# Where a chunk's state sums stand among the products of a Mamba-2 and MLP kernel on one core

## The chip, the core and the metric

The kernel runs on one core of one Trainium2 chip. A core has five engines that run side by side, each through its own queue in order: TensorE (PE in the profile; its weight loads are shown apart as PEld), VectorE (DVE), ScalarE (ACT), GpSimd (POOL) and the queue that issues transfers (SP). TensorE writes its products into PSUM, eight banks of 128 partitions by 512 fp32 words; VectorE and ScalarE read them there; everything else lies in SBUF. The metric is the time of one execution on the device, in microseconds, as the median of several runs.

## What is computed

A state-space layer (batch 4, 8 heads, 768 tokens, head size 32, state size 16) is followed by an MLP with a hardswish (256 to 2048 to 256), all in fp32 (the MLP's weights come as float64):

```python
for c in range(nc):                       # chunks of tokens
    cum = np.cumsum(la, axis=-1)          # la: log of the decay a
    L = np.exp(cum[:, :, :, None] - cum[:, :, None, :]) * causal
    M = np.einsum('bhin,bhjn->bhij', Cc, Bc) * L
    y_intra = np.einsum('bhij,bhjd->bhid', M, xc)
    y_inter = np.einsum('bhin,bhnd->bhid', Cc, state) * np.exp(cum)[..., None]
    y[:, :, sl] = y_intra + y_inter
    state = decay_full * state + sum_j(decay_from_j * Bc_j * xc_j)
...
h = x @ w_in                              # x: y with heads side by side
g = h * np.clip(h + 3.0, 0.0, 6.0) / 6.0
out = g @ w_out
```

## The kernel before

The tokens are cut into six chunks of 128 per sequence (NC = 6), all four sequences at once, and each chunk into two halves of 64 tokens (index `a`). Six stages `k` run the MLP of chunk `k`; into each one the attention of the next chunk, `c = k + 1`, is woven. The whole order is written out by hand: the engines' queues hold the instructions in the order in which the program emits them, and only waits for data or for buffers come on top.

The attention of a chunk has these parts, each with its line in the profile:
- `scores` (L530): C times B for each pair of heads, into four PSUM banks f0 to f3, named cb. Its products use the array in tiles of 32 rows and 64 columns (32*64).
- `from_state(c, a)` (L503): C times a state, into the output y. Half 0 uses the state left by the chunk before (`state`), half 1 the state at the middle of the chunk (`mid`). 32 products, 32*64.
- `into_state` (L544): the state sums, B weighted with the decay (`bs`) times x, 32 products for a half, in tiles of 64 rows and 32 columns (64*32). They go into `sps[c]`, the second halves of the banks y0 and y1 (the first halves hold y of half 0). The profile calls these tiles y as well.
- `multiply` (L574, VectorE): L times the scores, four instructions, which frees f0 to f3.
- `new_state` (L554, VectorE, two instructions): makes `mid` from the sums of half 0 and `tmp`, the decayed old state (L403, GpSimd); in `renew`, with `later` (L587) and the copy `adds` of the sums of half 1 (`take`, L560, ScalarE), it makes the chunk's last `state`.
- `mix` (L604): L times x into y, 128 products, 64*32, half `u` of the heads by half; y of token half 1 lies in the banks f0 and f1 (`y2`).
- `split_y` (L683, L684, L686): ScalarE and VectorE take y apart into three fp32r parts, y_hi, y_lo and y_less, the first layer's operands.

Stage `k` has two spans. In the first, for f from 2 to 15, the first layer's products (L694) and the activation follow each other, with hidden blocks rotating through the banks f0 to f3, y0 and y1. In the second, `wide_units` gives the second layer as products of whole-array tiles (L893, 128*128) into the banks wa, wb (pool ps_o) and wc (f2), cut into fourteen units of eight products (as the profile counts them); VectorE and ScalarE add the three banks together (L933, L934, L945, L946, L952, L953, L961) and the results are turned (L907) and stored (L914). L946 reads wb, and the products of unit 12 go on adding to wb behind it. After unit `i` the loop may emit parts of the next chunk's attention:

```python
if i == (3 if c == TURN else 2):          # TURN = 2
    scores(c); multiply(c)                # and renew(c), for TURN at i == 4
if ahead < NC and 3 <= i < 7:
    decay_ends(ahead, i - 3)              # ScalarE's L385, GpSimd's bs, L396
if i == 6 and c in (TURN, TURN + 1):
    mix(c, (0,))
if i == (7 if c in (TURN, TURN + 1) else 6):
    results(c, ...)                       # mix and split_y
```

So in stages 1 to 4, small products of chunks 2 to 5 stand in TensorE's queue between whole-array products. `scores` also emits `from_state(c, 0)` and `into_state`, for chunk 2 half 0 only (half 1 follows at unit 4, in `renew`), for chunk 5 half 0 only (its last state isn't needed). For chunk 5 `from_state(5, 0)` is emitted after unit 1, ahead of its scores. At unit 9 VectorE turns the B and C of the chunk after next (`turn_all`: L465, L475, L481); after `results`, ScalarE raises the decay of the chunk after next (`from_start`, L389), and SP loads the decays of the chunk behind that (`rows`: L301, L308). GpSimd also sums gT for the second layer (`g_sums`, L797) and masks the decays (L158).

Buffers that matter: `bs`, `mid`, `tmp`, `adds`, `later` and `xt` have one buffer; `state`, `L` and `eto` (the decay from a chunk's start) have two.

Of the kernel before, what the change touches and what calls it, by code (L numbers as in the profile page):

```python
# [8 lines left out]
FP32 = mybir.dt.float32  # L9
# [12 lines left out]
def kernel(  # L22
# [25 lines left out]
    P = 128  # L48
    NB, NH, S, D = x.shape
    N = B.shape[-1]  # L50
    DM, DF = moe_w_in.shape[0], moe_w_out.shape[0]
    NC = S // P
# [6 lines left out]
    HT = P // 2  # L59
# [24 lines left out]
    TURN = 2  # L84
# [431 lines left out]
    def scores(c):  # L516

        bT, cT, _ = bTs[c]
        cbs[c] = [ps.tile([P, NB, 2, HT], FP32, name="cb", tag=f"f{q}") for q in range(NQ)]
        if c not in ys:
            own_banks(c)
        for b in range(NB):
            for a, rows in enumerate(HALF):
                for q in range(NQ):
                    pair = slice(32 * q, 32 * q + 32)
                    nc.tensor.matmul(  # L530
                        out=cbs[c][q][rows, b], lhsT=bT[pair, b, rows],
                        rhs=cT[pair, b, :, rows], start=(b == 0), stop=True,
                        tile_position=(32 * q, a * HT), skip_group_check=True)
        if c == TURN:
            from_state(c, 0)
        into_state(c, *range(2 if c not in (TURN, NC - 1) else 1))

    def into_state(c, *halves):
        xt, bs = xts[c], bss[c]
        for b in range(NB):  # L540
            for q in range(NQ):
                hs = slice(b * NH + 2 * q, b * NH + 2 * q + 2)
                for a in halves:
                    nc.tensor.matmul(  # L544
                        out=sps[c][a][32 * q:32 * q + 32, b],
                        lhsT=bs[HALF[a], hs].rearrange("s h n -> s (h n)"),
                        rhs=xt[HALF[a], hs].rearrange("s h d -> s (h d)"),
                        start=(c == 0 and b == 0), stop=True, tile_position=(a * HT, 32 * q),
                        skip_group_check=True)

    def new_state(t, sp, old):
        for u in range(2):
# [8 lines left out]

    def multiply(c):

        if c < NC - 1 and c != TURN:
            take(c)
        mids[c] = mid = att.tile([P, NB, 2 * D], FP32, name="mid", bufs=1)
        if c == 0:
            for t in range(2):
                nc.scalar.activation(
                    mid[:, :, t * D:(t + 1) * D], sps[c][0][:, :, t * D:(t + 1) * D], AF.Copy,  # L570
                    scale=parity[:, t:t + 1])
        for q in (2, 0, 1, 3) if c in (TURN, NC - 1) else range(NQ):
            hs = slice(2 * q, 2 * q + 2)
            nc.vector.tensor_tensor(  # L574
                out=Ls[c][:, :, hs], in0=Ls[c][:, :, hs], in1=cbs[c][q], op=ALU.mult)
            if c and c != TURN and q == 1:
                new_state(mid, sps[c][0], tmps[c])

    def renew(c):

        if c == TURN:
            into_state(c, 1)
            take(c)
            new_state(mids[c], sps[c][0], tmps[c])
        states[c] = att.tile([P, NB, 2 * D], FP32, name="state")
        later = att.tile([P, NB, 2 * D], FP32, name="later", bufs=1)
        nc.vector.tensor_tensor(  # L587
            out=later, in0=mids[c], in1=etos[c][:, :, P - 1:P].to_broadcast([P, NB, 2 * D]),
            op=ALU.mult)
        new_state(states[c], adds[c], later)  # L590

    def mix(c, parts=range(2)):


        xt = xts[c]
        if 0 in parts:
            ys[c].update({
                (1, u): ps.tile([P, NB, HT], FP32, name="y2", tag=f"f{u}") for u in range(2)})
        for u in parts:
            for b in range(NB):  # L600
                for h in range(u * HU, (u + 1) * HU):
                    for a, rows in enumerate(HALF):
                        d0 = D * (h % HU)
                        nc.tensor.matmul(  # L604
                            out=ys[c][a, u][d0:d0 + D, b], lhsT=xt[rows, b * NH + h],
                            rhs=Ls[c][rows, b, h], start=(b == 0 and a >= min(c, 1)), stop=True,
                            tile_position=(a * HT, d0), skip_group_check=True)
            if c == 0:
                from_state(c, 1, (2 * u, 2 * u + 1))
        if c and 1 in parts:  # L610
            from_state(c, 1)

    def keep(c):
# [353 lines left out]
        load_decay(c)  # L967
        load_eto(c)

    def results(c, parts=range(2)):  # L970
        mix(c, parts)
        if c == 1:
            keep(c)
        split_y(c)

    def decay_ends(c, b):
        decay(c, b)
# [72 lines left out]
    for k in range(NC):  # L1050
        gTs[k] = ffn.tile([P, NF, TB], FP32, name="gT")
        c, ahead = k + 1, k + 2
        if k == 0:
            for f in range(NF):
                mlp_in(k, f)
                for i in weave.get(f, []):
                    weights(i, 1)
                if f in (6, 8):
                    diff_exp(c, f // 2 - 3)
            rows(ahead)  # L1060
            weights(NP + 1, 1)
            weights(NP + 3, 1)
            weights(NP + 2, 3)
            sums, ins = weight_sums(), [in_parts(i) for i in range(NP)]
            outs_ = [split_out(i) for i in range(NP)]
            next(ins[0])
            w_more = {(1, 1): (0, 0, 1), (2, 1): (1, 1, 2)}
            for i in range(NP):
                for b in range(NB):
                    first_out(b, i, c)  # L1070
                    for n in w_more.get((i, b), ()):
                        next(ins[n])
                    if (i, b) == (2, 0):
                        conceal(ahead, 0)
                        conceal(ahead, 1)
                    if (i, b) == (0, 0):
                        weights(NP + 3, 1)
                        weights(NP + 2, 1)
                        weights(NP + 3, 3)
                    elif (i, b) == (1, 3):  # L1080
                        turn(c, 1)
                        wake(c)
                        turn(c, 0)
                        load_bc(ahead)
                    elif (i, b) == (2, 3):
                        decay(ahead, 0)
                        scores(c)
                        multiply(c)
                        decay(ahead, 1)
                        renew(c)  # L1090
                        next(ins[2])
                        next(ins[2])
                    elif (i, b) == (3, 1):
                        results(c)
                        decay(ahead, 2)
                    elif (i, b) == (3, 2):
                        decay(ahead, 3)
                        from_start(ahead)
                    elif (i, b) == (3, 3):
                        for q in range(NB):  # L1100
                            ends(ahead, q)
            lead_on(c)
            rows(ahead + 1)
            continue
# [22 lines left out]
        for f in range(2, NF):  # L1127
# [19 lines left out]
            if k == 1:  # L1147
                if f in (4, 5, 7):
                    next(ins[3])
                if f in (9, 11, 13):  # L1150
                    next(sums)
                if f == NF - 1:
                    turn_all(c)
        cross(k, NF - 2)
        for i, _ in enumerate(wide_units(k)):
            if i == 0:
                cross(k, NF - 1)
                factor(k, NF - 2)
                factor(k, NF - 1)
                for n in range(4):  # L1160
                    for j in range(len(g_done.get(k, [])) * 2, NJ, 2):
                        g_sums(k, j, (n,))
                if k == 1:
                    next(sums)
            if c < NC:
                if i == 1 and c == NC - 1:
                    own_banks(c)
                if i == (3 if c == TURN else 2):
                    scores(c)
                    multiply(c)  # L1170
                    if c < NC - 1 and c != TURN:
                        renew(c)
                if i == 4 and c == TURN:
                    renew(c)
                if ahead < NC and 3 <= i < 7:
                    decay_ends(ahead, i - 3)
                if i == 6 and c in (TURN, TURN + 1):
                    mix(c, (0,))
                if i == (7 if c in (TURN, TURN + 1) else 6):
                    results(c, (1,) if c in (TURN, TURN + 1) else range(2))  # L1180
                    if ahead < NC:
                        from_start(ahead)
                    if ahead + 1 < NC:
                        rows(ahead + 1)
# [39 lines left out]
```

## Time and profile before

| | us |
|---|---|
| median of 3 runs | 342.09 |
| lowest and highest run | 342.03 and 343.32 |
| the profiled execution | 341.78 |
| its span in the profile | 340.0 |
| TensorE busy | 332.4 |
| VectorE busy | 238.8 |
| ScalarE busy | 198.6 |
| GpSimd busy | 125.0 |
| the second spans of stages 1 to 4 | 32.07, 31.63, 31.26, 31.27 |

The profile shows one execution. Times in it run from the start of its span; the execution's own time holds 1.8 us more around the span. Instructions on TensorE overlap, and the ends of matmuls are modelled, so what a row of products costs is read from the start of its first product to the start of the next row. A duration in the timeline is that of a merged row, to the modelled end of its last instruction.

### The profile page before, as it was taken

Reading aid. Unit: us, or ns where it says so; the run is one execution under the profiler, and the core shown is the slowest. Engines: PE = TensorE matmul, PEld = TensorE weight load, DVE = VectorE, ACT = ScalarE, POOL = GpSimd, SP = SyncE. Lnnn points to the kernel's source line nnn. Section 1 sums busy time; section 2 is a strip of 40 time slices with the busy share of each in tenths; the row PEclk is TensorE's granted clock in tenths of the full one; section 3 lists DMA queues with packets and bytes.
Section 4 is the critical chain, followed back from the end, with each engine's and each line's share of the span. In section 5 each row is a group of like instructions: output and inputs, shape, how many; then the busy total and the mean of one; then the engine's idle time right before and its main releaser. Section 6 shows DMA issues by size and latency. Waiting matters only on the chain.

```text
span 340.0 us, 8193 instructions
## 1 busy us (share of the span) xinstructions
PE 332.4 (98%) x3336; PEld 265.1 (78%) x3336; DVE 238.8 (70%) x380; ACT 198.6 (58%) x416; POOL 125.0 (37%) x123
## 2 busy tenths in 40 slices
PE   6999999999999999999999999999999999999995
PEld 2654448888888888888888888888888888899994
DVE  6699999997499859565528555537476445599973
ACT  4778878667986470676470576470586030677661
POOL 3300000280283897099813089920079700000000
PEclk9999999999999999999999999999999999999999
DMA  8999977052690216176007176001160001110001
GB/s 174 173 312 187 201 258 154 2 60 70 158 122 5 59 54 122 29 89 66 21 17 156 28 90 66 22 3 17 29 79 2 2 2 17 28 19 2 1 2 62
DMA packets 89605, 25.15 MB, mean 74 GB/s; under 512 B 82208, under 2 KB 85952, under 8 KB 89056
## 3 DMA queue, kind: packets, MB, share of 16 engines
q1 hardware_dynamic: 85184, 23.33, 37.3%
q10 hardware_dynamic: 4384, 1.31, 1.9%
q8 instruction: 26, 0.43, 0.5%
q14 instruction: 11, 0.09, 0.1%
HBM read 21.33 MB, written 3.29 MB: 72 GB/s over the span
## 4 chain that ended last, share of the span: by engine, by line
PE 94%; DMA 3%; DVE 1%; SPq 1%; issue 0%; DVEq 0%
PE h L694 33%; PE wb L893 13%; PE wc L893 8%; PE o L751 8%; PE h L626 8%; PE wa L893 8%; PE o L858 4%; PE y L604 3%; PE o_less L858 2%; PE y L503 2%; PE cb L530 2%; DMA raw<-in_moe_w_in_dram 2%; PE y L544 1%; DMA pairs<-in_C_dram 1%; SPq L101 1%; PE o_less L863 1%
## 5 line engine op out<-in xcount | busy, mean ns | idle before, releaser
L738 DVE SCALAR_TENSOR_TENSOR gT<-gT,h 128x512 f32<-128x512 f32 x96 | 64.8, 685 | 33.7 <-ACT gT L733 32.2
L733 ACT ACTIVATE gT<-h,half 128x512 f32<-128x512 f32 x96 | 65.1, 684 | 25.7 <-PE h L694 23.7
L714 ACT ACTIVATE h<-h 128x512 f32<-128x512 f32 x66 | 38.2, 585 | 39.0 <-PE h L694 38.7
L694 PE MATMUL h<-y_hi,w_part 128*128 128x512 f32 x160 | 51.5, 407 | 0.0
L694 PE MATMUL h<-y_less,w_part 128*128 128x512 f32 x160 | 50.1, 399 | 0.0
L694 PE MATMUL h<-y_lo,w_part 128*128 128x512 f32 x160 | 49.5, 395 | 0.0
L797 POOL TENSOR_TENSOR s<-gT 128x512 f32<-128x512 f32 x16 | 23.7, 1485 | 47.6 <-DVE gT L738 47.6
L694 PEld LDWEIGHTS h<-y_lo,w_part 128*128 128x128 f32 x160 | 30.0, 188 | 7.4
L694 PEld LDWEIGHTS h<-y_hi,w_part 128*128 128x128 f32 x160 | 30.0, 188 | 6.7 <-DVE gT L738 0.2
L694 PEld LDWEIGHTS h<-y_less,w_part 128*128 128x128 f32 x160 | 29.2, 188 | 6.0 <-ACT h L714 0.2
L385 ACT ACTIVATE L<-L,cum_n 128x64 f32<-128x64 f32 x128 | 31.6, 339 | 0.0
L751 PE MATMUL o<-w_out,gT 128*128 128x256 f32 x128 | 28.8, 381 | 0.0
L626 PE MATMUL h<-yT,w_in 128*128 128x512 f32 x64 | 27.7, 594 | 0.0
L751 PEld LDWEIGHTS o<-w_out,gT 128*128 128x128 f32 x128 | 24.1, 190 | 3.8 <-issue 0.5
L158 POOL TENSOR_SCALAR_AFFINE_SELECT L<-L 64x1024 f32<-64x1024 f32 (+1 forms) x16 | 20.4, 1281 | 10.4 <-PE h L694 5.1
L626 PEld LDWEIGHTS h<-yT,w_in 128*128 128x128 f32 x64 | 12.1, 190 | 14.9 <-issue 13.2
L574 DVE TENSOR_TENSOR L<-L,cb 128x512 f32<-128x512 f32 x24 | 15.2, 682 | 12.0 <-PE cb L530 12.0
L403 POOL TENSOR_TENSOR tmp<-state,eto 128x256 f32<-128x256 f32 x5 | 4.1, 820 | 53.1 <-ACT eto L389 50.1
L797 POOL TENSOR_TENSOR s<-gT,s 128x512 f32<-128x512 f32 x16 | 21.3, 1340 | 0.9
L396 POOL TENSOR_TENSOR bs<-B,L 128x128 f32<-128x128 f32 x24 | 11.7, 502 | 26.1 <-ACT L L385 21.4
L858 PE MATMUL o<-v_pair,g_pair 128*128 128x256 f32 x120 | 21.1, 281 | 0.0
L797 POOL TENSOR_TENSOR gT<-gT 128x512 f32<-128x512 f32 x16 | 20.6, 1294 | 0.9
(137 smaller groups left out, 593.8 us busy)
## 6 DMA issues: line engine op xcount, KB each, us to landing
raw<-in_moe_w_out_dram SPq DMA_DIRECT2D x4, 1024.0 KB
L<-cum_d SPq DMA_DIRECT2D x8, 512.0 KB
xt<-in_x_dram SPq DMA_DIRECT2D x6, 512.0 KB
raw<-in_moe_w_in_dram SPq DMA_DIRECT2D x3, 1024.0 KB
out_dram<-back SPq DMA_DIRECT2D x128, 16.0 KB
pairs<-in_C_dram SPq DMA_DIRECT2D x40, 32.0 KB
eto<-cum_e SPq DMA_DIRECT2D x20, 64.0 KB
B<-in_B_dram SPq DMA_DIRECT2D x5, 256.0 KB
```

Source lines behind the costliest of these rows:

```text
L158: nc.gpsimd.affine_select(out=t[rows], in_=t[rows], pattern=pattern, compare_op=ALU.is_ge, fill=-1e5, base=base, channel_multiplier=-1)
L385: nc.scalar.activation(Ls[c][:, b, h], Ls[c][:, b, h], AF.Exp, bias=cum_n[:, c, g:g + 1])
L574: nc.vector.tensor_tensor(out=Ls[c][:, :, hs], in0=Ls[c][:, :, hs], in1=cbs[c][q], op=ALU.mult)
L626: nc.tensor.matmul(out=h, lhsT=w_in[f // FP][:, j, f % FP * P:(f % FP + 1) * P], rhs=yTs[k][:, j].rearrange("p b i -> p (b i)"), start=(j ...
L694: nc.tensor.matmul(out=hs_[k, f], lhsT=w[j][:, f % FP * P:(f % FP + 1) * P], rhs=y[:, j], start=(start and j == 0), stop=True, skip_group_ ...
L714: nc.scalar.activation(h, h, AF.Copy, scale=1.0 / EPS + 1.0)
L733: nc.scalar.activation(gTs[k][:, f], h, AF.Relu, bias=half, scale=1.0 / 6.0)
L738: nc.vector.scalar_tensor_tensor(out=g, in0=g, scalar=1.0, in1=h, op0=ALU.min, op1=ALU.mult)
L751: nc.tensor.matmul(out=o[:, b % 2], lhsT=gTs[0][:, f, b * P:(b + 1) * P], rhs=w_out[:, f], start=(f == 0 and b % 2 == 0), stop=True, skip_ ...
L797: nc.gpsimd.tensor_tensor(out=o, in0=p_, in1=q_, op=op)
L858: nc.tensor.matmul(out=o[n // 2][b], lhsT=g_parts[t][n][:, b * P:(b + 1) * P], rhs=w, start=(t == 0 and b % 2 == 0 and n != 1), stop=True, ...
L893: nc.tensor.matmul(out=bank[:, slot], lhsT=lhs[:, j], rhs=rhs[:, j], start=(clear and j == 0), stop=True, skip_group_check=True)
```

## The change

For chunks 3 to 5 the state sums leave `scores` and are emitted, in the new function `sums`, directly ahead of the mixing; for chunk 2 only the sums of half 1 move there, from `renew`. The mixing is emitted undivided for chunks 2 and 3 as well. `from_state(5, 0)` is emitted with chunk 5's scores.

The sums need other places in PSUM. Those of half 1 lie in the second half of bank f0 (`more`), beside y of token half 1 and the first half of the heads, a bank that the mixing also writes; the sums' first product clears it in place of the mixing's (`start`). Those of half 0 of chunks 3 to 5 lie in bank f3. For chunks 3 to 5 `mid` is made from them by VectorE while the mixing is in TensorE's queue. `take` and `renew` of chunks 2 to 4 are emitted behind `split_y`. The results of chunk 4 are emitted after unit 5, before after unit 6; those of chunks 2 and 3 still after unit 7, and of chunk 5 after unit 6. The rest of the diff renames a generator, since `sums` is now a function's name.

```diff
@@ -533,10 +533,14 @@
                         tile_position=(32 * q, a * HT), skip_group_check=True)
         if c == TURN:
             from_state(c, 0)
-        into_state(c, *range(2 if c not in (TURN, NC - 1) else 1))
+        if c <= TURN:
+            into_state(c, *range(1 if c == TURN else 2))
 
     def into_state(c, *halves):
         xt, bs = xts[c], bss[c]
+        own = c > TURN, c >= TURN
+        if c > TURN:
+            sps[c][0] = ps.tile([P, NB, 2 * D], FP32, name="sp", tag="f3")
         for b in range(NB):
             for q in range(NQ):
                 hs = slice(b * NH + 2 * q, b * NH + 2 * q + 2)
@@ -545,8 +549,8 @@
                         out=sps[c][a][32 * q:32 * q + 32, b],
                         lhsT=bs[HALF[a], hs].rearrange("s h n -> s (h n)"),
                         rhs=xt[HALF[a], hs].rearrange("s h d -> s (h d)"),
-                        start=(c == 0 and b == 0), stop=True, tile_position=(a * HT, 32 * q),
-                        skip_group_check=True)
+                        start=(b == 0 and (c == 0 or own[a])), stop=True,
+                        tile_position=(a * HT, 32 * q), skip_group_check=True)
 
     def new_state(t, sp, old):
         for u in range(2):
@@ -561,9 +565,10 @@
 
     def multiply(c):
 
-        if c < NC - 1 and c != TURN:
+        if c < TURN:
             take(c)
-        mids[c] = mid = att.tile([P, NB, 2 * D], FP32, name="mid", bufs=1)
+        if c <= TURN:
+            mids[c] = mid = att.tile([P, NB, 2 * D], FP32, name="mid", bufs=1)
         if c == 0:
             for t in range(2):
                 nc.scalar.activation(
@@ -573,15 +578,23 @@
             hs = slice(2 * q, 2 * q + 2)
             nc.vector.tensor_tensor(
                 out=Ls[c][:, :, hs], in0=Ls[c][:, :, hs], in1=cbs[c][q], op=ALU.mult)
-            if c and c != TURN and q == 1:
+            if 0 < c <= TURN and q == 1:
                 new_state(mid, sps[c][0], tmps[c])
 
-    def renew(c):
-
+    def sums(c):
+
+        if c < NC - 1:
+            own_halves(c, 1)
+            sps[c][1] = ys[c].pop("more")
         if c == TURN:
             into_state(c, 1)
-            take(c)
-            new_state(mids[c], sps[c][0], tmps[c])
+            return
+        into_state(c, *range(2 if c < NC - 1 else 1))
+        mids[c] = att.tile([P, NB, 2 * D], FP32, name="mid", bufs=1)
+        new_state(mids[c], sps[c][0], tmps[c])
+
+    def renew(c):
+
         states[c] = att.tile([P, NB, 2 * D], FP32, name="state")
         later = att.tile([P, NB, 2 * D], FP32, name="later", bufs=1)
         nc.vector.tensor_tensor(
@@ -589,25 +602,33 @@
             op=ALU.mult)
         new_state(states[c], adds[c], later)
 
-    def mix(c, parts=range(2)):
+    def own_halves(c, more=0):
+
+        for u in range(2):
+            t = ps.tile([P, 1 + more * (1 - u), NB, HT], FP32, name="y2", tag=f"f{u}")
+            ys[c][1, u] = t[:, 0]
+            if u < more:
+                ys[c]["more"] = t[:, 1]
+
+    def mix(c):
 
 
         xt = xts[c]
-        if 0 in parts:
-            ys[c].update({
-                (1, u): ps.tile([P, NB, HT], FP32, name="y2", tag=f"f{u}") for u in range(2)})
-        for u in parts:
+        if (1, 0) not in ys[c]:
+            own_halves(c)
+        more = c in range(TURN, NC - 1)
+        for u in range(2):
             for b in range(NB):
                 for h in range(u * HU, (u + 1) * HU):
                     for a, rows in enumerate(HALF):
                         d0 = D * (h % HU)
                         nc.tensor.matmul(
                             out=ys[c][a, u][d0:d0 + D, b], lhsT=xt[rows, b * NH + h],
-                            rhs=Ls[c][rows, b, h], start=(b == 0 and a >= min(c, 1)), stop=True,
+                            rhs=Ls[c][rows, b, h], start=(b == 0 and a >= min(c, 1) and u >= more), stop=True,
                             tile_position=(a * HT, d0), skip_group_check=True)
             if c == 0:
                 from_state(c, 1, (2 * u, 2 * u + 1))
-        if c and 1 in parts:
+        if c:
             from_state(c, 1)
 
     def keep(c):
@@ -967,11 +988,16 @@
         load_decay(c)
         load_eto(c)
 
-    def results(c, parts=range(2)):
-        mix(c, parts)
+    def results(c):
+        if c >= TURN:
+            sums(c)
+        mix(c)
         if c == 1:
             keep(c)
         split_y(c)
+        if TURN <= c < NC - 1:
+            take(c)
+            renew(c)
 
     def decay_ends(c, b):
         decay(c, b)
@@ -1061,7 +1087,7 @@
             weights(NP + 1, 1)
             weights(NP + 3, 1)
             weights(NP + 2, 3)
-            sums, ins = weight_sums(), [in_parts(i) for i in range(NP)]
+            more, ins = weight_sums(), [in_parts(i) for i in range(NP)]
             outs_ = [split_out(i) for i in range(NP)]
             next(ins[0])
             w_more = {(1, 1): (0, 0, 1), (2, 1): (1, 1, 2)}
@@ -1148,7 +1174,7 @@
                 if f in (4, 5, 7):
                     next(ins[3])
                 if f in (9, 11, 13):
-                    next(sums)
+                    next(more)
                 if f == NF - 1:
                     turn_all(c)
         cross(k, NF - 2)
@@ -1161,23 +1187,15 @@
                     for j in range(len(g_done.get(k, [])) * 2, NJ, 2):
                         g_sums(k, j, (n,))
                 if k == 1:
-                    next(sums)
+                    next(more)
             if c < NC:
-                if i == 1 and c == NC - 1:
-                    own_banks(c)
                 if i == (3 if c == TURN else 2):
                     scores(c)
                     multiply(c)
-                    if c < NC - 1 and c != TURN:
-                        renew(c)
-                if i == 4 and c == TURN:
-                    renew(c)
                 if ahead < NC and 3 <= i < 7:
                     decay_ends(ahead, i - 3)
-                if i == 6 and c in (TURN, TURN + 1):
-                    mix(c, (0,))
-                if i == (7 if c in (TURN, TURN + 1) else 6):
-                    results(c, (1,) if c in (TURN, TURN + 1) else range(2))
+                if i == {TURN: 7, TURN + 1: 7, TURN + 2: 5}.get(c, 6):
+                    results(c)
                     if ahead < NC:
                         from_start(ahead)
                     if ahead + 1 < NC:
```

## The prediction

> **What bounds the kernel now.** I read the page first, then the chain that ended last, then TensorE's timeline in the stretches where a chunk's attention work lies between the output products of the chunk before, and last VectorE's and GpSimd's timelines there. The page:
>
> ```profile
> PE 332.4 (98%) x3336; PEld 265.1 (78%) x3336; DVE 238.8 (70%) x380; ACT 198.6 (58%) x416; POOL 125.0 (37%) x123
> ...
> PEclk9999999999999999999999999999999999999999
> ...
> PE 94%; DMA 3%; DVE 1%; SPq 1%; issue 0%; DVEq 0%
> ```
>
> TensorE is busy 98% of the span, is 94% of the chain, and has its full clock throughout. So the time is what TensorE's queue costs plus any wait put into it. From 84.8 us on the chain is TensorE until the last output product. The change only touches the stretches of chunks 2 to 5: 105.50 to 137.57, 157.75 to 189.38, 209.53 to 240.79 and 260.93 to 292.20 us, or 32.07, 31.63, 31.26 and 31.27 us. Chunk 2's, and a part of chunk 4's and of chunk 5's, in TensorE's timeline (start, duration, line, output<-inputs, rows*columns of the array in use):
>
> ```profile
> 114.71 1.99 PE L893 MATMUL wc<-gT,w_out 128*128 128x256 f32 x8
> 116.64 0.65 PE L544 MATMUL y<-xt,bs 64*32 64x64 f32 x32
> 117.22 1.99 PE L893 MATMUL wc<-gT,w_out 128*128 128x256 f32 x8
> 119.05 0.59 PE L893 MATMUL wa<-gT,w_out 128*128 128x256 f32 x2
> 119.48 1.89 PE L893 MATMUL wb<-s,t 128*128 128x256 f32 x8
> 121.30 0.86 PE L604 MATMUL y<-L,xt 64*32 64x64 f32 x64
> ...
> 125.43 3.72 PE L893 MATMUL wc<-gT,t 128*128 128x256 f32 x16
> 128.98 3.62 PE L893 MATMUL wa<-s,t 128*128 128x256 f32 x16
> ...
> 223.07 1.89 PE L893 MATMUL wb<-s,t 128*128 128x256 f32 x8
> 224.89 1.48 PE L604 MATMUL y<-L,xt 64*32 64x64 f32 x128
> ...
> 264.50 0.69 PE L503 MATMUL y<-csT,state 32*64 32x64 f32 x32
> 265.13 1.99 PE L893 MATMUL wb<-gT,t 128*128 128x256 f32 x8
> ```
>
> The reader is to see start-to-start times. Small products on a part of the array (64*32, 32*64) stand between products on the whole array (128*128), and each such stretch costs more than its products. From 114.71 to 119.05, 16 wc products with one small stretch among them take 4.34; the 16 from 125.43 to 128.98, also just behind a small stretch, take 3.55. So the 32 small products cost 0.79, of which 0.58 is their own start-to-start time (116.64 to 117.22) and 0.2 slower whole-array products before and behind. The undivided mixing of chunk 4 shows the same price: wb, mixing, L503 and wc take 223.07 to 232.21, 9.14, and in chunk 2, divided by eight wb products, 119.48 to 128.98, 9.50. One stretch less is 0.36.
>
> **TensorE's part of the change.** The number of matmuls stays; stretches go, and changes between two small shapes. A change from one small shape to another costs about 0.15: 64 mixing products in a stretch of their own take 0.79 (121.30 to 122.09), 128 take 1.41 (224.89 to 226.30), so the second 64 add 0.62 and the rest, 0.16, is leaving the shape. State sums (L544) and mixing (L604) have the same shape, 64*32, so sums put directly ahead of the mixing cost their products alone.
> - Chunk 2: the stretch of 32 state sums goes, -0.79; they return ahead of the mixing at 0.58 less 0.15, +0.43; the mixing is undivided, -0.36. Sum -0.72.
> - Chunk 3: its 64 sums leave the scores' stretch (0.79, 164.66 to 165.44) and return for 0.64, -0.15; undivided mixing -0.36. Sum -0.51.
> - Chunk 4: only the sums move, -0.15 (its mixing was undivided; it comes eight products earlier, which costs nothing here).
> - Chunk 5: the stretch of 32 state products at 264.50 goes: 0.63 (to 265.13) and the 0.2 around, -0.83. With the scores they cost what chunk 3's state products and scores take (163.05 to 164.66, 1.61) less chunk 5's scores alone (267.05 to 268.19, 1.14): +0.47. Its 32 sums -0.15. Sum -0.51.
> Together -1.89; the records round to 0.01, but the 0.15 could be 0.10 in each of four places, so 1.7 to 2.0; I take 1.85.
>
> **What else moves, and its cover.** (a) New wait on mid: for chunks 3 to 5 VectorE must make mid (two L554, 0.60 together) between the sums and the L503 products, while the mixing runs (1.41). 0.8 is used with the semaphores, 0.6 is left. VectorE must be free then: in chunk 5 it works off two L822 from 275.10 to 276.38, which move 0.9 earlier with TensorE and end 0.4 before the sums do. Cost 0; if VectorE were late, its lateness less 0.5. (b) ACT's copy of the sums (L560, 0.37) goes behind the four y_hi copies; ACT waits 2.48 for wc after that. 0. (c) bs has one buffer, so GpSimd's four bs products for the next chunk (L396) now wait for this chunk's sums, some 5 us later in chunk 3 (first at 168.18 before). Behind them lie tmp (L403) and the masking (L158); GpSimd then idles 11.51 before 196.86. 0. (d) SP: the four eto loads of the chunk after next (L308) wait for VectorE's last read of eto, the product later (L587), now after the mixing. In chunk 2 that moves their issue from 126.17 to about 130.2; behind them are 32 stores (19.32 us of issue), then x, B and C. x was issued at 148.16 and comes up to 4 later; its first reader is at 172 or after. The B and C pairs are first read by the transposes at 182.0. 0. (e) VectorE's own renewal of the state (L587, two L554), 1.4 to 3.5, moves from before the mixing to behind y_less, ahead of L946, which reads wb and must be done before TensorE goes on with wb. This is where I see a price:
>
> ```profile
> 118.00 2.45 DVE L554 SCALAR_TENSOR_TENSOR state<-adds,parity,later 128x128 f32<-128x128 f32 x2
> ...
> 168.61 0.61 DVE L554 SCALAR_TENSOR_TENSOR state<-adds,parity,later 128x128 f32<-128x128 f32 x2
> ...
> 129.37 1.97 POOL L396 TENSOR_TENSOR bs<-B,L 128x128 f32<-128x128 f32 x4
> ```
>
> In chunk 2 the state pair took 2.45 (first row), and the two y_less instructions (L686) 3.34, where chunk 3 has 0.61 (second row) and 1.71: GpSimd was summing gT beside them (up to 129.41) and both engines read SBUF. The third row is what GpSimd does next. After the change y_less, which ended at 129.96, ends 0.7 earlier with TensorE, at 129.27. With later at 0.81, the pair at 0.61 and L946 at 0.68, L946 ends at 131.4; TensorE wants wb at 132.44 less 0.7, 131.74: no wait, the lower end. With 1.03 and 2.45 as in chunk 2's own rows it ends at 133.4: 1.7 of waiting, the upper end. Nearest is the work that GpSimd has just then: the sums end, and four bs products of 0.41 follow. Each of the pair can then wait for one of these: later to its follower 0.91 (167.70 to 168.61), the pair 0.61 + 0.82, L946 0.68, done at 132.3. I take 0.5 of waiting. In chunk 3 the same gives 181.8 against 183.75 (GpSimd idle), in chunk 4 more room still: 0. Behind L946 VectorE's backlog in chunk 2 is eaten by its idle 1.11 and 1.02 before 137.96 and 140.15.
>
> The Trainium skill, "SBUF — State Buffer", section "Who interferes with whom", says that a VectorE instruction with two SBUF inputs and a GpSimd instruction that reads SBUF exclude each other, the second to issue waiting until the first is finished. It speaks against moving these three next to GpSimd's work; by that rule the engines take turns, which for this stretch also leads to about 0.5, and the trace agrees with it in the pair's 2.45 against 0.61.
>
> **Sum.** -1.85 + 0.5 = -1.35. The profiled execution took 341.78 (span 340.0); it becomes 340.4. The median of the runs, 342.09, is 0.31 above it, and I forecast on it: 340.7, faster by 0.4%.
>
> **The rivals.** (1) No wait on wb: GpSimd is done sooner or its products fall between VectorE's. For it: L946 ends at 131.4 by uncontended rows. Against it: y_less is contended in the same place. 342.09 - 1.85 = 340.2, faster by 0.54%. (2) The long wait: the pair meets late gT sums, as chunk 2's did, 1.2 to 1.7 on wb; 341.6 to 342.0, no change. For it: the row of 2.45; against it, the sums end at 129.4. (3) On the other side: mid comes late. If VectorE reaches the two L554 of chunks 3 to 5 only after work that is queued ahead of them (the sum L934 behind ACT's copy, or L822), TensorE stands before L503. The gain is gone when the three waits sum to 1.35, and it is slower by over 0.5% when they sum to 3.1, each mid 1.0 behind the end of the mixing, so done 2.4 after the sums instead of 0.8; 343.9 with such waits. Against it: L934 ended at 223.76 in chunk 4 and moves 0.8 earlier, the sums end at 223.0. (4) The shapes don't merge: if the sums and the mixing do not run on without a break, because they write other banks, then each of the four places gives 0.15 back, 0.6 in all: 341.3, no change. Against it: the L544 products alternate between two banks now at 10 ns each (64 in 0.79, 0.15 of it leaving the shape).
>
> **How the numbers follow.** A measurement of this kernel tells about 0.5% (1.71) from no change. Forecast (wait 0.2 to 0.9) 0.52; rival 1, 0.23; rival 2, 0.11; rival 4, 0.06; rival 3, 0.08. The forecast's own range is 340.3 to 341.2. Faster by over 0.5% is rival 1 and a sliver: 0.25. Slower is rival 3: 0.08. The rest, 0.67, is within. The range leaves rival 3 out, and runs from 2.0 gained and no wait, less the 0.3 that executions differ by, 339.8, to the long wait, 342.1.
>
> **What would show it.** Stretches of 31.9, 31.1, 31.1 and 30.8 for the four chunks; two small stretches in each of them; L544 followed by L604 without a pause; a wait of some 0.5 before the wb products near 131.7, released by L946, and state's pair over 1 us there. Wrong would be a pause before L503 in chunks 3 to 5 (rival 3), no pause at 131.7 (rival 1), or the last stretch still above 31.

## The result, and the profile after

The changed kernel takes 341.35 us (median of 15 runs) against 342.25 us for the kernel before (15 runs). The ratio is 0.9963, with a 95% interval from 0.9945 to 0.998: 0.37% faster. The forecast was 340.7 us and 0.4%, from 339.8 to 342.1. The profiled execution took 341.63 us (span 339.5). The size came out right, partly by luck: two terms of the sum were wrong, in opposite directions.

The windows view of the kernel after, one line for each stretch (from the first wa product of a stage to the first product behind its last wb products; start and end, length, then each engine's busy time):

```profile
106.75:138.10 31.35, 31.35 (x444) 27.18 (x442) 22.89 (x35) 14.72 (x47) 24.56 (x21) 1.00 0.28 64
158.24:189.54 31.30, 31.23 (x443) 26.70 (x442) 16.45 (x30) 13.47 (x45) 14.72 (x16) 1.00 0.31 64
209.68:241.00 31.32, 31.25 (x444) 26.70 (x442) 15.35 (x30) 13.26 (x45) 12.38 (x14) 1.00 0.10 19
261.18:291.97 30.79, 30.79 (x411) 26.60 (x410) 14.86 (x28) 5.96 (x13) 8.88 (x8) 1.00 0.05 9
```

| stretch of chunk | before | forecast, TensorE's own part | measured | gain |
|---|---|---|---|---|
| 2 | 32.07 | -0.72, and a wait of 0.5 | 31.35 | 0.72 |
| 3 | 31.63 | -0.51 | 31.31 | 0.33 |
| 4 | 31.26 | -0.15 | 31.32 | -0.06 |
| 5 | 31.27 | -0.51 | 30.79 | 0.48 |
| sum | 126.23 | -1.89 + 0.5 | 124.76 | 1.47 |

(The last line is the sum of the windows view; single entries are rounded.) Everything between the stretches takes TensorE the same time as before, to 0.05 us. In chunks 3 and 4 TensorE is idle for 0.07 in the rows, where before it never was. Its timeline for chunk 2, and for the scores of chunk 3 (start, duration, line, output<-inputs, rows*columns):

```profile
115.96 3.72 PE L914 MATMUL wc<-gT,w_out 128*128 128x256 f32 x16
...
123.50 0.48 PE L548 MATMUL y<-xt,bs 64*32 64x64 f32 x20
123.77 0.24 PE L625 MATMUL y<-L,xt 64*32 64x64 f32 x1
...
123.94 1.47 PE L625 MATMUL y<-L,xt 64*32 64x64 f32 x124
125.34 0.69 PE L503 MATMUL y<-csT,mid 32*64 32x64 f32 x32
125.96 3.72 PE L914 MATMUL wc<-gT,t 128*128 128x256 f32 x16
129.52 3.62 PE L914 MATMUL wa<-s,t 128*128 128x256 f32 x16
132.97 1.89 PE L914 MATMUL wb<-s,w_out 128*128 128x256 f32 x8
...
165.14 1.99 PE L914 MATMUL wb<-gT,t 128*128 128x256 f32 x8
167.20 3.72 PE L914 MATMUL wc<-gT,w_out 128*128 128x256 f32 x16
```

Chunk 2 is as forecast: one stretch of sums is gone, and sums and mixing run into each other without a break (their order in the rows overlaps by a few products). From wa at 129.52 to wb at 132.97 is 3.45, the plain time of 16 products: the wait of 0.5 is not there. VectorE's sum that reads wb (L967, L946 in the kernel before) ends at 132.59, 0.38 ahead:

```profile
131.91 0.68 DVE L967 TENSOR_TENSOR wide<-wb,third 128x512 f32<-128x512 f32 x1
```

Chunk 3 holds what the forecast had missed. Eight wb products take 1.84 when nothing follows them late (165.63 to 167.47 in the first experiment); here wc starts 2.06 after wb.

The chain of waits over the same place, in order of time (start, duration, what):

```profile
164.23 1.03 PE cb L530 x55
165.26 0.01 issue
165.27 1.89 DVE L L579 x3
167.16 0.04 issue
167.20 3.72 PE wc L914 x16
```

TensorE's weight loads, which otherwise run ahead of the products, name the same releaser:

```profile
167.20 3.32 PEld L914 LDWEIGHTS wc<-gT,w_out 128*128 128x128 f32 x16 [0.47 <-DVE L L579]
```

VectorE is on the chain. wc lies in bank f2, the third of the four banks that VectorE's L times scores products read one after the other (L579). In the kernel before, the 64 sums stood between the scores and these whole-array products, and covered most of that reading; I had moved them and counted only their own price.

Last, the first 23 us. The change doesn't touch them, and yet the first wa product starts 1.25 later than before (106.75 against 105.50). The chain of waits of the kernel after shows most of it as one pause inside chunk 0's mixing:

```profile
19.26 0.85 PE y L625 x51
20.11 1.15 issue
21.25 0.31 PE y L625 x6
```

"issue" is a wait that the profile can put down to nothing. The kernel before has 0.02 in this place. So of the 1.47 gained in the stretches, these two single executions show hardly any: 341.78 against 341.63.

A part of that loss lies outside the profile. In every run of the kernel before and of its two variants that has its span on record (e3_undivided and e6_ch5 below), the time holds 1.72 to 1.83 us more than the span. In every run of the kernel after and of its variants it holds 2.11 to 2.22 more, with one exception, the single run of e8_unit_6, with 1.76. So the change pays nearly 0.4 us where no view looks. The cause is open; that it hangs on the place of chunk 4's results, the only line in which e8_unit_6 differs from e1_order, is one run's hint and not shown.

### The profile page after: what moved, and what is told of

Its sections match the earlier page's. It is cut to its first block, busy times and chain, and to the rows that moved or that the text cites. A ratio compares the mean times of both kernels' runs of the same rounds, so it can differ in the third digit from the quotient of the medians.

```text
span 339.5 us, 8188 instructions
## 1 busy us (share of the span) xinstructions
PE 330.6 (97%) x3336; PEld 265.0 (78%) x3336; DVE 235.0 (69%) x380; ACT 199.1 (59%) x416; POOL 124.0 (37%) x123
## 4 chain that ended last, share of the span: by engine, by line
PE 93%; DMA 3%; DVE 2%; SPq 1%; issue 1%; DVEq 0%
PE h L715 33%; PE wb L914 11%; PE wc L914 8%; PE o L772 8%; PE h L647 8%; PE wa L914 8%; PE o L879 4%; PE y L625 3%; PE o_less L879 2%; PE y L503 2%; PE cb L530 2%; DMA raw<-in_moe_w_in_dram 2%; DVE L L579 1%; DMA pairs<-in_C_dram 1%; PE y L548 1%; SPq L101 1%
## 5 line engine op out<-in xcount | busy, mean ns | idle before, releaser
L579 DVE TENSOR_TENSOR L<-L,cb 128x512 f32<-128x512 f32 x24 | 15.1, 683 | 11.6 <-PE cb L530 11.6
L403 POOL TENSOR_TENSOR tmp<-state,eto 128x256 f32<-128x256 f32 x5 | 3.2, 642 | 53.9 <-ACT eto L389 50.0
L396 POOL TENSOR_TENSOR bs<-B,L 128x128 f32<-128x128 f32 x24 | 11.0, 482 | 29.9 <-ACT L L385 21.3
```

What stands on the lines that cost most here:

```text
L579: nc.vector.tensor_tensor(out=Ls[c][:, :, hs], in0=Ls[c][:, :, hs], in1=cbs[c][q], op=ALU.mult)
```

## The experiments

Lengths of stretches are read like those above. Lines of code are those of the kernel after where nothing else is said.

**The order in which VectorE reads the banks (e1_order).** Theory A says that TensorE waits for f2, theory B that the change of shape costs more than I took.

```diff
-        for q in (2, 0, 1, 3) if c in (TURN, NC - 1) else range(NQ):
+        for q in (2, 0, 1, 3) if c >= TURN else range(NQ):
```

> The kernel after, with the order 2, 0, 1, 3 of VectorE's four L times scores products in chunks 3 and 4 as well, so that bank f2 is read first. Theory A: in the kernel after, TensorE waits 0.23 us before the first wc product in each of chunks 3 and 4, because the state sums no longer stand behind the scores and VectorE has not yet read f2 (its third of four products). Then both waits go: the stretches of chunks 3 and 4 become 31.08 us each, after 31.31 and 31.32, and the whole 0.46 us shorter than the kernel after, about 0.5% below the kernel before. Theory B: the missing 0.2 us in each is the price of a change of shape, larger than the 0.15 that I took: then the wait stays and nothing changes.

Chunk 2 takes 31.39 us, chunks 3 and 4 30.98 each, chunk 5 30.80. TensorE's rows for the same place in chunk 3:

```profile
165.63 2.00 PE L914 MATMUL wb<-gT,t 128*128 128x256 f32 x8
167.47 3.62 PE L914 MATMUL wc<-gT,w_out 128*128 128x256 f32 x16
170.92 0.60 PE L914 MATMUL wa<-gT,w_out 128*128 128x256 f32 x2
```

The wait is gone, with no matmul moved: theory A holds, B falls. The gain is 0.33 a chunk, not 0.23. Beside the wait of 0.22, the 16 wc products take 3.45 here (167.47 to 170.92) and 3.56 in the kernel after (167.20 to 170.76), 0.11 more. The trace has all of this in the first product behind the wait: the next one starts 0.32 behind it, where 0.22 is usual. Its weights are loaded only as it starts (167.20), and without the wait 0.22 ahead of it (167.25 in e1_order); that this is the reason is argued. The median is 340.88 us (6 runs) against 343.09 (11) for the kernel before on the same chip, ratio 0.993 (0.9913 to 0.9947).

**The sums of chunks 3 and 4 back among the scores (e2_sums_back).** mid, the copy and the renewal go back with them; only the mixing stays undivided.

```diff
-        if c <= TURN:
+        if c < NC - 1:
             into_state(c, *range(1 if c == TURN else 2))
...
-        more = c in range(TURN, NC - 1)
+        more = c == TURN
```

> The kernel after, with the sums of chunks 3 and 4 back among their scores (and mid, the copy and the new state back beside them), the mixing undivided, chunk 4's results still after unit 5. Theory A: no wait before wc, as the sums cover VectorE's products: chunk 3 31.27 us (before, 31.63, less 0.36 for the undivided mixing), chunk 4 31.26 as before. So moving the sums of these two chunks would have cost 0.04 and 0.06 as it was done. Theory B: the undivided mixing brings less than 0.36 and moving the sums is not at fault: chunk 3 at 31.4 or more, chunk 4 at 31.3.

31.26 and 31.27 us, as theory A has it. So in the change as it was made, moving these two chunks' sums cost 0.05 each. With the order mended as well, each chunk gains 0.29 (31.26 to 30.98), where I had forecast 0.15 for the sums. About half of this is not the sums' but the order's: f2 already cost a little in the kernel before. Its chunk 3, which reads f2 third, beside its chunk 5, which reads it first:

```profile
165.44 1.99 PE L893 MATMUL wb<-gT,t 128*128 128x256 f32 x8
167.33 3.69 PE L893 MATMUL wc<-gT,w_out 128*128 128x256 f32 x16
170.86 0.59 PE L893 MATMUL wa<-gT,w_out 128*128 128x256 f32 x2
...
268.77 1.99 PE L893 MATMUL wb<-gT,t 128*128 128x256 f32 x8
270.60 3.62 PE L893 MATMUL wc<-gT,w_out 128*128 128x256 f32 x16
274.05 0.59 PE L893 MATMUL wa<-gT,w_out 128*128 128x256 f32 x2
```

From start to start, wb and wc take 1.89 and 3.53 in chunk 3, and 1.83 and 3.45 in chunk 5: 0.14 together. That leaves 0.15 for the sums. The new order with the sums still among the scores was not run, so this split is worked out, not measured.

**The undivided mixing alone, in the kernel before (e3_undivided).**

```diff
-                if i == 6 and c in (TURN, TURN + 1):
-                    mix(c, (0,))
...
-                    results(c, (1,) if c in (TURN, TURN + 1) else range(2))
+                    results(c)
```

> The kernel before with the mixing of chunks 2 and 3 undivided after unit 7, and nothing else. By the price of a stretch, 0.36 us, chunk 2 takes 31.71 and chunk 3 31.27 us, chunks 4 and 5 31.26 and 31.27 as before. Rival: the y parts come later, since ScalarE can start on the first half of y only when both halves of the mixing are done, and TensorE waits for them ahead of the first layer's products: chunks 2 and 3 stay near 32.07 and 31.63.

31.71, 31.27, 31.27 and 31.29 us: 0.36 in chunk 2 and 0.37 in chunk 3, none of it lost to a later y. The one run took 343.2 us, against a median of 343.09 before, although 0.7 is gone from the stretches: its first wa product starts at 107.60, 2.1 later than in the profile before. A single time says nothing at this size; the stretches do.

**Chunk 5's state products alone, in the kernel before (e6_ch5).** `own_banks(5)` emits `from_state(5, 0)`; without this call `scores` does it.

```diff
-                if i == 1 and c == NC - 1:
-                    own_banks(c)
```

> The kernel before with chunk 5's 32 state products emitted with its scores, and nothing else: 0.83 us less for the stretch that goes, 0.47 more among the scores, so 30.91 for chunk 5, and 32.07, 31.63 and 31.26 as before for the others. Rival: the products now stand ahead of the scores, VectorE's products for wc's bank come later, and TensorE waits there: 31.1 to 31.3.

32.05, 31.61, 31.25 and 30.92 us: 0.35 in chunk 5, as forecast. Of the 0.48 that chunk 5 gains in the kernel after, 0.13 is then left for its sums, where the forecast had 0.15. Here VectorE already read f2 first, and 32 sums still stood behind the scores.

**All of chunk 2's sums ahead of its mixing (e7_all_of_2).** Built on e1_order; the half that stood behind chunk 2's scores moves too, and chunk 2's `mid` is then made while the mixing runs, as in chunks 3 to 5.

```diff
-        if c <= TURN:
-            into_state(c, *range(1 if c == TURN else 2))
+        if c < TURN:
+            into_state(c, 0, 1)
...
-        own = c > TURN, c >= TURN
+        own = c >= TURN, c >= TURN
```

> The kernel e1_order with the other half of chunk 2's sums moved ahead of its mixing too. In chunk 2 the wc products follow the scores at once, without eight wb products between them as in chunks 3 and 4. Theory A (the sums behind the scores cover VectorE's reading of f2): the sums' 0.58 us go, TensorE then waits about 0.45 for f2, restarts at a cost of 0.1, and the 32 sums cost 0.2 ahead of the mixing: chunk 2 at about 31.5 us, no better than 31.35. Rival (state sums are always cheaper ahead of the mixing): 30.97. The others 30.98, 30.98 and 30.80.

Chunk 2 takes 31.42 us, the others 30.98, 30.98 and 30.79. TensorE's rows and VectorE's behind chunk 2's scores:

```profile
115.03 0.71 PE L503 MATMUL y<-csT,state 32*64 32x64 f32 x31
116.11 3.72 PE L911 MATMUL wc<-gT,w_out 128*128 128x256 f32 x16 [0.37 <-DVE L L579]
```

```profile
115.37 2.48 DVE L579 TENSOR_TENSOR L<-L,cb 128x512 f32<-128x512 f32 x4 [1.02 <-PE cb L530]
```

wc follows the scores at once here, and even with f2 read first (115.37 to some 116.05) it waits. So moving the 32 sums that stay with chunk 2's scores gains nothing: they fill the time in which VectorE reads the bank.

**Chunk 4's results after unit 6 (e8_unit_6).** Built on e1_order.

```diff
-                if i == {TURN: 7, TURN + 1: 7, TURN + 2: 5}.get(c, 6):
+                if i == {TURN: 7, TURN + 1: 7}.get(c, 6):
```

> The kernel e1_order with chunk 4's results after unit 6, as in the kernel before, in place of unit 5. Nothing that TensorE waits for should change: chunk 4 at 30.98 us either way. Rival: the earlier place is worth something (a part of y that the first layer's products wait for, or mid): chunk 4 above 31.1.

31.36, 30.98, 30.98 and 30.79 us. The place of chunk 4's results is worth nothing to TensorE. (The time outside the span, 1.76 here, is told of above.)

**More work ahead of L967 in chunk 2 (e4_dve_more).** The kernel after; does the sum that reads wb (L946 before, L967 after) hold TensorE, as the forecast's wait of 0.5 supposed?

```diff
-        new_state(states[c], adds[c], later)
+        for _ in range(3 if c == TURN else 1):
+            new_state(states[c], adds[c], later)
```

> The kernel after, with chunk 2's new state written three times over, the same values: four L558 instructions more on VectorE between y_less and L967. In the kernel after, L967 ended 0.4 us before TensorE needed wb. If L967 does hold TensorE's wb products, as the prediction has it, the four instructions (1.0 us where GpSimd leaves them alone, up to 1.6 beside its bs products) bring a wait of 0.7 to 1.2 us before these products, and chunk 2's stretch grows from 31.35 to about 32.0 to 32.6 us. Rival: wb is not held by L967, and the stretch stays at 31.35.

Chunk 2 takes 32.55 us, 1.20 more. VectorE's rows, and TensorE's:

```profile
130.50 2.13 DVE L558 SCALAR_TENSOR_TENSOR state<-adds,parity,later 128x128 f32<-128x128 f32 x6
132.56 0.68 DVE L968 TENSOR_TENSOR wide<-wb,third 128x512 f32<-128x512 f32 x1
```

```profile
128.81 3.62 PE L915 MATMUL wa<-s,t 128*128 128x256 f32 x16
133.38 1.97 PE L915 MATMUL wb<-s,w_out 128*128 128x256 f32 x8 [0.95 <-POOL tmp L403]
```

The three pairs take 2.13 where one took 0.77 in the kernel after, 1.36 more, and wb starts 4.57 behind wa in place of 3.45, 1.12 late and 0.14 behind the end of L968 (133.24). The row names GpSimd's tmp as the releaser, but tmp only reads the state that VectorE finished shortly before, and nothing of it goes to wb. In the kernel after, wb starts at 132.97 while tmp runs until 133.20, so wb doesn't wait for it. L968 is what is left. So the path is real, and the kernel after stands about 0.24 short of paying on it: 1.36 of work more made wb 1.12 late.

**The kernel after once more (e5_again).**

> The kernel after, unchanged, once more, to hold its time against the kernel before on this chip and its profile against the first one. The stretches of chunks 2 to 5 should come out at 31.35, 31.31, 31.32 and 30.79 us again. In the first profile TensorE also stood still for 1.2 us inside chunk 0's mixing near 20 us, in code that the change doesn't touch, and not so in the profile of before; if that differs from execution to execution, this profile shows another value, between 0 and 1.4 us.

31.35, 31.31, 31.31 and 30.79 us; median 341.6 (9 runs) against 343.1 (14), ratio 0.995 (0.9921 to 0.9979). There is no pause in chunk 0's mixing in this execution. Yet its first layer starts at 23.46, as in the first profile (23.50), since its scores of chunk 0 ran later. In the profiles of this study the first wa product starts anywhere from 105.50 to 107.60.

**mid made late in chunk 4 (e9_mid_late).** Built on e1_order; a test of the third rival, that TensorE could stand before the products that read mid.

```diff
-        new_state(mids[c], sps[c][0], tmps[c])
+        for _ in range(3 if c == TURN + 2 else 1):
+            new_state(mids[c], sps[c][0], tmps[c])
```

> The kernel e1_order with chunk 4's mid written three times over, the same values: four L558 instructions more on VectorE while the mixing runs. In the kernel after, mid was done some 0.5 us before TensorE reached the products that read it. If those products do wait for mid, as the third rival of the prediction has it, the four instructions (1.0 to 1.2 us, the bank lies in PSUM, so GpSimd doesn't disturb them) make TensorE wait 0.5 to 0.8 before them, and chunk 4 takes 31.5 to 31.8 in place of 30.98 us. Rival: VectorE has more room than that, and chunk 4 stays under 31.2. Chunks 2, 3 and 5 as in e1_order: 31.4, 30.98, 30.80.

Chunk 4 takes 31.58 us, 0.60 more than in e1_order:

```profile
226.29 0.69 PE L503 MATMUL y<-csT,mid 32*64 32x64 f32 x32 [0.54 <-DVE mid L558]
```

1.03 of work more, 0.54 of waiting: mid has about 0.5 to spare, and the rival's path is real but not taken. The surprise is chunk 2, which the edit doesn't touch: 32.97 us, 1.58 more than in e1_order. VectorE's first y_less there took 4.8 us, where one alone takes 0.68.

**Chance in VectorE's turn (e11_order_again and e10_renew_late).** To see whether that was an accident, e1_order ran again unchanged, beside a version of it in which chunk 2's renewal stands behind L967:

```diff
-            renew(c)
+            if c > TURN:
+                renew(c)
...
+                if i == 9 and c == TURN:
+                    renew(c)
```

> The kernel e1_order, unchanged, once more, beside e10_renew_late. By theory C its chunk 2 shows 31.35 to 31.4, or again about 33; chunks 3 to 5 30.98, 30.98 and 30.79. Ratio to the kernel before about 0.993 or 0.994.

> The kernel e1_order with chunk 2's renewal (later and the two state instructions) emitted after unit 9, behind L946's successor and ahead of the turning of B and C. In e9_mid_late, whose code is the same up to there, chunk 2 took 32.97 us in place of 31.39: VectorE's first y_less waited 4.8 us beside GpSimd's sums, and TensorE waited 1.5 us before wb. Theory C: VectorE's turn beside GpSimd is a matter of chance in each execution, and what stands between y_less and the reading of wb decides how much of it TensorE pays. Then chunk 2 is at 31.35 here, or at most at about 31.6 in an execution where y_less is late; the median against the kernel before is the same as e1_order's 0.993 or up to 0.1% lower. Rival: the 32.97 came from e9's own edit and chance plays no part: no difference from e1_order in chunk 2, 31.39 in both, and in their times.

e11_order_again is the same program as e1_order, and in its profile chunk 2 takes 32.99 us (30.97, 30.97 and 30.80 for the others). Chunk 2 in e1_order, VectorE and GpSimd:

```profile
127.62 2.50 DVE L707 SCALAR_TENSOR_TENSOR y_less<-y_lo,y_hi 128x512 fp32r<-128x512 f32 x2
130.05 1.49 DVE L600 TENSOR_TENSOR later<-mid,eto 128x256 f32<-128x256 f32 x1
131.65 0.77 DVE L558 SCALAR_TENSOR_TENSOR state<-adds,parity,later 128x128 f32<-128x128 f32 x2
132.35 0.68 DVE L967 TENSOR_TENSOR wide<-wb,third 128x512 f32<-128x512 f32 x1
...
125.40 5.85 POOL L818 TENSOR_TENSOR s<-gT,s 128x512 f32<-128x512 f32 x4
131.22 1.85 POOL L396 TENSOR_TENSOR bs<-B,L 128x128 f32<-128x128 f32 x4
```

And in e11_order_again, with TensorE's wb:

```profile
127.42 5.42 DVE L707 SCALAR_TENSOR_TENSOR y_less<-y_lo,y_hi 128x512 fp32r<-128x512 f32 x2
133.97 0.68 DVE L967 TENSOR_TENSOR wide<-wb,third 128x512 f32<-128x512 f32 x1
...
125.26 4.96 POOL L818 TENSOR_TENSOR s<-gT,s 128x512 f32<-128x512 f32 x4
130.16 1.54 POOL L396 TENSOR_TENSOR bs<-B,L 128x128 f32<-128x128 f32 x4
...
134.80 1.97 PE L914 MATMUL wb<-s,w_out 128*128 128x256 f32 x8 [1.39 <-POOL tmp L403]
```

In e1_order the two engines take turns and both are slowed (GpSimd's four sums 5.85). In e11_order_again GpSimd runs all its sums and bs products at full speed (4.96 and 1.54) and VectorE gets nothing until these are over, at 131.7. Then L967 ends at 134.65, and wb starts at 134.80, 5.01 behind wa at 129.79 in place of 3.45: 1.56 late. This is the wait of the forecast's second rival, 1.2 to 1.7, in the place that it named, but in some executions only, and by another instruction: y_less is held up, where the rival had the state pair, which takes 0.76 here. The profiles of e1_order and e11_order_again come from two chips, but that the chip decides is unlikely: e11's other five executions, on its own chip, were 1.5 to 2.3 us shorter than the profiled one, and e9's late y_less came on e1_order's chip. In the thirteen profiles here the pair y_less takes 2.48 to 2.54 in eight, 3.31 to 3.36 in three (the kernel before among them) and 5.38 and 5.42 in two. What decides it is not shown.

e10_renew_late has 31.36, 30.98, 30.97 and 30.79 us and 340.82 (6 runs) against 343.05 (11), ratio 0.9936 (0.9921 to 0.9951), e11_order_again 340.85 (6 runs), ratio 0.9947 (0.9927 to 0.9967). e11's profiled execution took 342.83, its other five 340.49 to 341.29; e10's six lie from 340.43 to 341.41. Since y_less was short in e10's profile (2.54), it doesn't show what a late one would cost there; that the version is safer is argued from the order of the queue, not shown. Both are faster than the kernel before. Their stretches of chunks 3 and 4 are shorter than the kernel after's; by whole times neither the comparison with the kernel after nor e10 against e1_order is settled, as the intervals overlap.

## Why the prediction was right, and where it was wrong

That 0.37% lies so near to 0.4% is in part luck. TensorE's own gain of 1.89 came out 0.42 short, a wait of 0.5 did not come, and these two cancel; the start of the kernel and the time outside the span then move an execution by more than what is left. The 341.35 us also lie above the 340.3 to 341.2 that the forecast gave its own sum, though the kernel before was 0.16 slower here too. By the forecast's own sign, no pause at 131.7, the profile after is its first rival; the TensorE gain of 1.85 in that rival's 340.2 us was 1.47.

- **What bounds the kernel.** Right. TensorE's queue is the time inside the stretches, and each part of their gain is found in its rows, whatever the whole execution shows.
- **A stretch less: 0.36 for the mixing, and as much for chunk 2's sums and chunk 5's state products.** Right. e3_undivided measured 0.36 and 0.37, e6_ch5 0.35 in chunk 5, and chunk 2 gained the forecast's 0.72.
- **"Chunk 3: ... -0.15" and "Chunk 4: only the sums move, -0.15".** This is the step that failed. The price of the products was right: 0.15 in chunks 3 and 4 and 0.13 in chunk 5 are left when the other parts are taken off. But I never asked what runs while TensorE works on them, and so put at nothing the wait that opens when they go. They hid VectorE's reading of f2. The wait of 0.22 and the late product behind it, 0.11, take 0.33 from each chunk (e1_order), where f2 had cost about 0.14 before; the 0.19 more is larger than the 0.15 gained, and moving the sums cost 0.05 (e2_sums_back).
- **Rival 4, the shapes don't merge.** Fell: L548 and L625 follow each other without a break.
- **The cover of mid, 0.6 to spare.** Right in kind, some 0.5 in size: e9_mid_late added 1.03 and got 0.54.
- **The wait of 0.5 on wb (e).** The path is right (e4_dve_more) and the size wrong, since it has no one size. In the profile after, L967 ended 0.4 before wb was wanted: y_less and the state pair took 2.54 and 0.77 in place of 3.34 and 1.43, and later 1.49 in place of 0.91. In two of the nine profiles with the renewal ahead of L967 the wait was about 1.5 (and 1.12 in e4_dve_more, which adds work there). The Trainium skill's rule ("SBUF — State Buffer", "Who interferes with whom"), that the second to issue waits until the first is finished, fits the executions in which the engines take turns. It does not fit the two others: there VectorE's y_less, which starts in the trace while one gT sum ran, was passed over by GpSimd's two later sums and all four bs products. Here the measurement decides: to wait for the one that runs is the best case.
- **The sum.** -1.85 + 0.5 = -1.35 against -1.47 in the stretches: 0.42 of the TensorE gain was missing, and 0.5 of waiting did not come in these executions. The sum also took the time outside the span as unchanged, without a reason; it grew by nearly 0.4.
- **SP, GpSimd's later bs products, ScalarE's copy, chunk 4's earlier place.** No cost in the stretches, as forecast; e8_unit_6 shows it for the last.

## What to carry to other kernels

Before an instruction is taken out from between two others on the engine that sets the time, ask what the other engines do meanwhile: a product that looks like a cost may be the cover under which a bank is read, and then the order of that reading has to move with it. Read small gains from stretches of the bounding engine's timeline that the edit touches; here they repeat to a few hundredths while whole executions differ by 1 to 2 us. And where two engines take turns at operands in SBUF, give what a third engine waits for room for the worst turn, since a mean of a few profiles doesn't show it.

## What the runs showed of the hardware that was not expected

- VectorE can lose its turn to GpSimd for a whole series: one y_less of 0.68 us alone took 4.8 beside GpSimd's sums and products at full speed (e11_order_again), in the same program that took 2.5 for two of them in another execution (e1_order).
- A wait of TensorE costs more than its length: behind the 0.22 the first whole-array product took 0.32 to the start of the next in place of 0.22, and the 16 together 3.56 in place of 3.45. The first one behind a stretch of small products shows the same 0.32 (the wb at 165.63 in e1_order).
- The start of the kernel, the same code in all versions, takes from 105.5 to 107.6 us up to the first wa product, with pauses of TensorE of up to 1.15 us that no semaphore or transfer in the profile explains. Their cause is open.
